# Attention with grouped heads on one core: the key order of VectorE's K transposes, and the pairs that use the wide PV

## The chip, the core and the metric

The kernel runs on one core of one Trainium2 chip. The metric is the device time of one execution in microseconds (us), and smaller is better. A core has engines that run their own instruction streams and meet through semaphores: TensorE (PE) multiplies matrices into PSUM, VectorE (DVE) and ScalarE (ACT) work on elements, GpSimd (POOL) does odd jobs, and SyncE (SP) issues the transfers between the device memory and the on-chip memory SBUF. The transfers are carried by 16 DMA engines.

## The reference

```python
B, Hq, Hkv, Sq, Sk, D = 16, 32, 8, 16, 2048, 128        # q, k, v in bf16

def reference(q, k, v):
    rep = Hq // Hkv                                      # 4 query heads share one K/V head
    k = jnp.repeat(k, rep, axis=1)
    v = jnp.repeat(v, rep, axis=1)
    scores = jnp.einsum("bhqd,bhkd->bhqk", q, k) * D ** -0.5
    p = _softmax(scores, axis=-1)
    return jnp.einsum("bhqk,bhkd->bhqd", p, v)
```

There are 16 x 8 = 128 K/V heads. Each has 2048 keys of 128 numbers and is met by 4 x 16 = 64 query rows. K and V together are 128 MB, and each of their numbers is used only by its own 64 rows.

## The kernel before

**Pairs.** Two K/V heads make a pair, so there are 64 pairs `p`. The 64 query rows of both heads fill the 128 partitions of the score tile. One pair goes through these steps:

1. SP loads 1 MB of K into `Kn` (L176) and 1 MB of V into `Vb` (L184). In `Kn` a partition holds 32 consecutive keys of one head, that is 16 keys for each of two values of `x`; in `Vb` a partition holds 16 consecutive keys of each head.
2. DVE transposes K in blocks of 32 x 32 four-byte words (function `kt`, L317, two instructions a pair, one for each `x`). A four-byte word is two neighbouring numbers of a key. The result is `KT`, in which the keys run along the free dimension. In the pattern on L318 the letters `(t b e a x)` say in which order the free dimension holds the pieces of a key's number: `t` and `e` are the index of a key within its 16 (`e` tells odd from even), `a` and `x` tell which 16, and `b` is a half of the head dimension.
3. PE multiplies `QT` with `KT` into `S_ps` (L268 and L224, 32 matmuls), 2048 scores in each of 128 rows.
4. DVE scales and negates the scores into `Sneg` in SBUF and takes the row's minimum in the same instruction (L333). It frees `S_ps`, of which there is one.
5. ACT takes exp into `P` in bf16, with the row sum (L368). Its pattern reads `Sneg` as `(n e y)` and writes `n y e`: from each group of 128 scores it takes turns between the 64 even keys and the 64 odd keys, so that an even and the following odd key lie side by side in `P` and can be moved as one four-byte word.
6. PE transposes those words of `P` in 8 blocks (L280), and ACT copies them to `PT` (L378).
7. PE multiplies `PT` with `Vb` (PV). In the wide form (L298) one matmul for each of 16 key groups uses all 128 rows of both heads as weights and both heads' V as 256 columns; half of the 128 x 256 result is of use. In the narrow form (L304) two matmuls for each key group, one for each head, with 64 rows and 128 columns, fill two halves of the array and give only what is needed. `NFAST` says how many of the last pairs use the narrow form: 12.
8. ACT multiplies by the reciprocal row sum and writes `Osb`: two instructions for the wide form (L391), one for the narrow form (L395). DVE does this for the last pair (L348). SP stores the result (L204).

Every eight pairs a new block of queries is spread by POOL (L165), transposed on PE (L246) and copied to `QT` by ACT (L358), in four parts behind four successive pairs.

**Order.** The streams of PE and ACT are written out as lists before the block: scores of pair `p + 1`, exp of pair `p`, PV and norm of pair `p - 3`, transposes of `P` of pair `p`. DVE does reduction `p`, the reciprocal of `p - 1` and the two K transposes of `p + 2`. SP issues K of step `t`, V of pair `t - 5` and the store of pair `t - 12` in one stream. There are 6 buffers for K, 8 for V and 2 for `KT`; the load of K of pair `p` waits for the transposes of pair `p - 6`, that of V for PV of pair `p - 8`. V of the last pair comes in two parts, of 12 and 4 key groups.

The lines that tie DVE's and PE's steps together are these:

```python
# PE, scores of pair p
pe.wait_ge(sem_kt, 2 * p + 2)
pe.wait_ge(sem_max, p)            # the one S_ps has been read
# DVE
dve.wait_ge(sem_s, p + 1)         # reduction of pair p
...
for g in range(2):
    kt(p + 2, g)
```

Of the kernel before, what the change touches and what calls it, by code (L numbers as in the profile page):

```python
# [5 lines left out]
ACT = mybir.ActivationFunctionType  # L6
ALU = mybir.AluOpType
BF16 = mybir.dt.bfloat16
# [5 lines left out]
NKT = 2  # L14
# [6 lines left out]
SLAG = 12  # L21
QLEAD = 7
LASTV = ((0, 12), (12, 16))
NFAST = 12


def bass_standalone__gqa_softmax__sampling_kernel(
# [12 lines left out]
    J = Sk // 128  # L40
# [13 lines left out]
    KT = [sb(f"KT{i}", [128, 2 * J * 64], F32) for i in range(NKT)]  # L54
# [3 lines left out]
    Sneg = [sb(f"Sneg{i}", [128, Sk], F32) for i in range(2)]  # L58
    P = [sb(f"P{i}", [128, Sk // 2], F32) for i in range(2)]
# [83 lines left out]
    def stage_ap(u):  # L143
        return ST_ps[:, 512 * (u % NSTAGE):512 * (u % NSTAGE + 1)]

    def o_ap(p):
        if p < NP - 3:
            return O_ps[:, 0:128]
        x = p - (NP - 3)
        return S_ps[:, 512 * x:512 * x + 128]  # L150

    with nc.Block() as block:

        @block.gpsimd
        def _(gp):
            gp.iota(iota_t[:, :], [[1, 128]], base=0, channel_multiplier=-1).then_inc(sem_id, 1)
            gp.wait_ge(sem_id, 1)
            gp.tensor_scalar(ident[:, :], iota_t[:, :], 0.0, None, op0=ALU.is_equal).then_inc(sem_id, 1)
            gp.tensor_scalar(ident4[:, :], iota_t[:, :], 0.0, None, op0=ALU.is_equal).then_inc(sem_id, 1)
            for c in range(NQC):  # L160
                gp.wait_ge(sem_q[c % NQ], 16 * (c // NQ + 1))
                if c >= 1:
                    gp.wait_ge(sem_st, last_q[c - 1, 3] + 1)
                src = Qn[c % NQ][:, :, :].rearrange("p j (b x) -> p (j b) x", b=2)
                gp.tensor_copy(  # L165
                    Q4[:, :, :, :, :].rearrange("p j b r x -> p (j b) r x"),
                    src.unsqueeze(2).to_broadcast([128, 16, 4, 64]),
                ).then_inc(sem_q4, 1)
# [51 lines left out]
        def _(pe):  # L220
# [15 lines left out]
            for op in pe_prog:  # L236
                if op[0] == "QT":
                    _, c, i, u = op
                    if i == 0:
                        pe.wait_ge(sem_q4, c + 1)  # L240
# [6 lines left out]
                    ins.then_inc(sem_st, 1)  # L247
                elif op[0] == "S":
                    _, p = op
                    pe.wait_ge(sem_kt, 2 * p + 2)  # L250
                    if p >= 1:
# [19 lines left out]
                    ins.then_inc(sem_s, 1)  # L271
                elif op[0] == "PT":
                    _, p, h, u = op
                    if h == 0:
                        pe.wait_ge(sem_exp, p + 1)
# [6 lines left out]
                elif op[0] == "PV":  # L282
# [9 lines left out]
                    for j in range(J):  # L292
                        if p == NP - 1:
                            for x, (lo, _) in enumerate(LASTV):
                                if j == lo:
                                    pe.wait_ge(sem_vl[x], 16)
                        if p < NP - NFAST:
                            ins = pe.matmul(  # L298
# [14 lines left out]
        @block.vector  # L313
        def _(dve):
            def kt(p, x):
                dve.wait_ge(sem_k[p % NK], 16 * (p // NK + 1))
                dve.transpose(  # L317
                    KT[p % NKT][:, :].rearrange("p (t b e a x) -> p x e t b a", t=J // 2, b=2, e=2, x=2)[:, x, :, :, :, :],  # L318
                    Kn[p % NK][:, :].bitcast(F32).rearrange("p (x t e b c) -> p x e t b c", x=2, e=2, b=2, c=32)[:, x, :, :, :, :],
                ).then_inc(sem_kt, 1)  # L320

            def recip(p):
                dve.wait_ge(sem_exp, p + 1)
                dve.reciprocal(rrec[:, p:p + 1], rowsum[:, p:p + 1]).then_inc(sem_rec, 1)  # L324

            for p in range(2):
                for g in range(2):
                    kt(p, g)
            for p in range(NP):
                dve.wait_ge(sem_s, p + 1)  # L330
                if p >= 2:
                    dve.wait_ge(sem_exp, p - 1)
                dve.tensor_scalar(  # L333
                    Sneg[p % 2][:, :].rearrange("p (t h x) -> p h t x", t=8, h=2),
                    S_ps[:, :].rearrange("p (h t x) -> p h t x", t=8, h=2), -scale, None,
                    op0=ALU.mult, op1=ALU.min, accum_out=nbias[:, p:p + 1],
                ).then_inc(sem_max, 1)
                if p >= 1:
                    recip(p - 1)
                if p + 2 < NP:  # L340
                    for g in range(2):
                        kt(p + 2, g)
            recip(NP - 1)
            p = NP - 1
            dve.wait_ge(sem_rec, NP)
            dve.wait_ge(sem_o[p % NO], 16 * (p // NO))
            dve.wait_ge(sem_pv, NP)
            dve.tensor_scalar(Osb[p % NO][:, :], o_ap(p), rrec[:, p:p + 1], None, op0=ALU.mult).then_inc(sem_nl, 1)  # L348

        @block.scalar  # L350
        def _(act):
            for op in act_prog:
                if op[0] == "qe":
                    _, c, i, u = op
                    act.wait_ge(sem_st, u + 1)
                    if c >= 2 and i == 0:
                        act.wait_ge(sem_s, 8 * (c - 1))
                    act.activation(  # L358
                        QT[c % 2][:, i // 2, :].rearrange("p (a x j) -> p x a j", x=2, j=4)[:, i % 2],
                        stage_ap(u).rearrange("p (j a) -> p a j", j=4), ACT.Copy,  # L360
                    ).then_inc(sem_ev, 1)
                elif op[0] == "exp":
                    _, p = op
                    act.wait_ge(sem_max, p + 1)
                    if p >= 2:
                        act.wait_ge(sem_st, last_p[p - 2, 1] + 1)

                    act.activation(  # L368
                        P[p % 2][:, :].bitcast(BF16).rearrange("p (n y e) -> p n y e", n=16, e=2),
                        Sneg[p % 2][:, :].rearrange("p (n e y) -> p n y e", n=16, e=2), ACT.Exp,  # L370
                        bias=nbias[:, p:p + 1], scale=-1.0, accum_out=rowsum[:, p:p + 1],
                    ).then_inc(sem_exp, 1)
                elif op[0] == "pe":
                    _, p, h, u = op
                    act.wait_ge(sem_st, u + 1)
                    if h == 0 and p >= NPT:
                        act.wait_ge(sem_pv, p - NPT + 1)
                    act.activation(  # L378
                        PT[p % NPT][:, 4 * h:4 * (h + 1), :].rearrange("p t q -> p (t q)"),
                        stage_ap(u), ACT.Copy,  # L380
                    ).then_inc(sem_ev, 1)
                else:
                    _, p = op
                    act.wait_ge(sem_pv, p + 1)
                    act.wait_ge(sem_rec, p + 1)
                    if p >= NO:
                        act.wait_ge(sem_o[p % NO], 16 * (p // NO))
                    if p < NP - NFAST:
                        for g in range(2):
                            rows = slice(64 * g, 64 * (g + 1))  # L390
                            ins = act.activation(Osb[p % NO][rows, :], O_ps[rows, 128 * g:128 * (g + 1)], ACT.Copy,  # L391
                                                 scale=rrec[rows, p:p + 1])
                        ins.then_inc(sem_nm, 1)
                        continue
                    act.activation(Osb[p % NO][:, :], o_ap(p), ACT.Copy,  # L395
                                   scale=rrec[:, p:p + 1]).then_inc(sem_nm, 1)
# [28 lines left out]
```

## Time and profile before

| | |
|---|---|
| time, median of 3 runs | 344.95 us (344.94 to 345.17) |
| the profiled execution: its own time | 344.92 us |
| its span, first to last instruction | 343.1 us |
| busy: PE, DVE, ACT | 312.1, 297.6, 291.8 us |
| exp, L368, 64 of them | 2481 ns each |
| K transposes, L317, 128 of them | 1218 ns each |
| reductions, L333, 64 of them | 2285 ns each |
| moved by DMA | 138.94 MB, mean 405 GB/s |

An execution takes 1.8 us more than the span that the profile covers. In the profile's rows a group is named by its line, engine, operation and tiles, with its busy time and the mean duration of one instruction; "idle before" is the time that the engine stood before instructions of the group, and the name behind the arrow says what ended it. In rows by slice each digit is a fortieth of the span. Rows in order of time begin with the start and the duration in us; a bracket gives the idle time before the instruction. Rows by stretch give the busy time of each engine, then the granted clock of PE as a share of full speed, the busy share of the DMA engines and GB/s.

### The profile page before, as it was taken

How to read it: one execution, taken by the hardware profiler on the slowest of the kernel's cores; microseconds unless marked ns; L12 is line 12 of the kernel's file. 1: busy time of each engine (PE TensorE's matmuls, PEld its weight loads, DVE VectorE, ACT ScalarE, POOL GpSimd, SP SyncE). 2: the span in 40 equal slices, each digit the busy share in tenths (PEclk: the TensorE clock that was granted, in tenths of full speed). 3: DMA queues.
4: the chain of work that ended last, by engine and by line, in shares of the span. 5: the costliest groups of instructions: out<-in, count | busy, mean ns of one | idle time of the engine just before them, and what ended most of it. 6: DMA issues, size and time to landing. Idle time of an engine off the chain costs nothing.

```text
span 343.1 us, 8217 instructions
## 1 busy us (share of the span) xinstructions
PE 312.1 (91%) x3904; PEld 189.2 (55%) x2880; DVE 297.6 (87%) x321; ACT 291.8 (85%) x404; POOL 30.3 (9%) x15
## 2 busy tenths in 40 slices
PE   0757999999999999999999999999999999887784
PEld 0413656655665575557555755665565575454354
DVE  2289989999999999999899989998999898989840
ACT  1258899999999999999999999999988899877864
POOL 4500012000400004000300004000040000000000
PEclk9999999999999999999999999999999999999999
DMA  7999999999999999999999999999999999999993
GB/s 294 429 414 415 415 411 413 414 416 417 412 418 419 413 415 417 412 420 415 412 421 414 414 416 416 415 418 417 415 412 419 419 412 420 417 413 418 410 393 126
DMA packets 37300, 138.94 MB, mean 405 GB/s; under 512 B 11408, under 2 KB 11664, under 8 KB 29072
## 3 DMA queue, kind: packets, MB, share of 16 engines
q1 hardware_dynamic: 37264, 138.42, 99.6%
q8 instruction: 27, 0.44, 0.5%
q14 instruction: 9, 0.07, 0.1%
HBM read 136.31 MB, written 2.10 MB: 403 GB/s over the span
## 4 chain that ended last, share of the span: by engine, by line
PE 83%; DMA 5%; issue 4%; DVE 3%; ACT 1%; SPq 1%; POOL 1%; DVEq 0%; ACTq 0%
PE O_ps L298 28%; PE S_ps L268 18%; PE S_ps L224 15%; PE ST_ps L280 15%; PE ST_ps L246 5%; DMA Vb<-in_v_dram 4%; DVE KT L317 2%; PE O_ps L304 2%; DMA Qn<-in_q_dram 1%; DVE Sneg L333 1%; POOL Q L165 1%; SPq L204 1%; ACT P L368 1%; SPq L184 0%; PE S_ps L304 0%
## 5 line engine op out<-in xcount | busy, mean ns | idle before, releaser
L333 DVE TENSOR_SCALAR_CACHE_REDUCE Sneg<-S_ps 128x2048 f32<-128x2048 f32 x64 | 146.2, 2285 | 25.2 <-PE S_ps L224 24.0
L368 ACT ACTIVATE P<-Sneg,nbias 128x2048 bf16<-128x2048 f32 x64 | 158.8, 2481 | 7.7 <-DVE Sneg L333 6.1
L317 DVE STREAM_TRANSPOSE KT<-Kn 128x1024 f32<-128x1024 f32 x128 | 150.9, 1218 | 10.9 <-DMA Kn<-in_k_dram 10.9
L268 PE MATMUL S_ps<-KT,QT 32*64 32x512 bf16 x1024 | 103.4, 391 | 5.5 <-DVE Sneg L333 4.7
L224 PE MATMUL S_ps<-KT,QT 32*64 32x512 bf16 x1024 | 102.0, 385 | 0.0
L298 PEld LDWEIGHTS O_ps<-Vb,PT 128*128 128x128 bf16 x832 | 77.3, 98 | 44.0 <-issue 35.7
L298 PE MATMUL O_ps<-Vb,PT 128*128 128x256 bf16 x832 | 99.9, 273 | 1.5 <-issue 1.5
L378 ACT ACTIVATE PT<-ST_ps 128x512 f32<-128x512 f32 x128 | 69.5, 595 | 6.0 <-PE ST_ps L280 4.8
L280 PE MATMUL ST_ps<-ident,P 128*128 128x128 f32 x512 | 69.0, 278 | 2.8 <-ACT P L368 2.8
L268 PEld LDWEIGHTS S_ps<-KT,QT 32*64 32x64 bf16 x1024 | 30.0, 104 | 70.4 <-issue 61.6
L280 PEld LDWEIGHTS ST_ps<-ident,P 128*128 128x128 f32 x512 | 55.1, 141 | 12.1 <-ACT P L368 9.6
L391 ACT ACTIVATE O<-O_ps,rrec 64x128 bf16<-64x128 f32 x104 | 37.7, 363 | 15.8 <-PE O_ps L298 14.7
L165 POOL COPY Q<-Qn 128x4096 bf16<-128x4096 bf16 x8 | 28.8, 3602 | 224.2 <-PE ST_ps L246 143.9
L246 PE MATMUL ST_ps<-ident,Q 128*128 128x128 f32 x128 | 20.4, 291 | 10.1 <-POOL Q L165 10.1
L358 ACT ACTIVATE QT<-ST_ps 128x512 f32<-128x512 f32 x32 | 19.3, 603 | 10.0 <-PE ST_ps L246 10.0
L246 PEld LDWEIGHTS ST_ps<-ident,Q 128*128 128x128 f32 x128 | 16.4, 150 | 10.1 <-issue 10.1
L304 PE MATMUL O_ps<-Vb,PT 128*64 128x128 bf16 x288 | 9.8, 220 | 7.2 <-issue 7.2
L304 PEld LDWEIGHTS O_ps<-Vb,PT 128*64 128x64 bf16 x288 | 8.5, 110 | 12.9 <-issue 12.9
L324 DVE RECIPROCAL rrec<-rowsum 128x1 f32<-128x1 f32 x64 | 10.1, 158 | 3.1 <-ACT P L368 3.1
L368 ACT ACTIVATION_READ_ACCUMULATOR P<-Sneg,nbias 128x1 f32 x64 | 12.2, 190 | 0.0
L395 ACT ACTIVATE O<-O_ps,rrec 128x128 bf16<-128x128 f32 x9 | 3.3, 365 | 6.6 <-PE O_ps L304 6.6
L333 DVE DVE_READ_ACCUMULATOR Sneg<-S_ps 128x1 f32 x64 | 5.3, 83 | 0.0
(12 smaller groups left out, 10.2 us busy)
## 6 DMA issues: line engine op xcount, KB each, us to landing
Kn<-in_k_dram SPq DMA_DIRECT2D x64, 1024.0 KB, 15.9
Vb<-in_v_dram SPq DMA_DIRECT2D x63, 1024.0 KB, 17.7
Qn<-in_q_dram SPq DMA_DIRECT2D x8, 256.0 KB, 15.6
out_dram<-O SPq DMA_DIRECT2D x64, 32.0 KB, 15.9
Vb<-in_v_dram SPq DMA_DIRECT2D x1, 768.0 KB, 13.0
Vb<-in_v_dram SPq DMA_DIRECT2D x1, 256.0 KB, 12.5
```

What stands on the lines that cost most here:

```text
L165: gp.tensor_copy(Q4[:, :, :, :, :].rearrange("p j b r x -> p (j b) r x"), src.unsqueeze(2).to_broadcast([128, 16, 4, 64]),).then_inc(sem_q ...
L224: return pe.add_instruction(mybir.InstMatmult(name=nc.get_next_instruction_name(), engine=mybir.EngineType.PE, ins=[pe.lower_ap(rhs), pe.l ...
L246: ins = pe.transpose(dst[:, 128 * j:128 * (j + 1)], src[:, 4 * x + j, b, :], ident4[:, :])
L268: ins = pe.matmul(s_ap, w, x, start=(acc == 0), stop=(acc == 3))
L280: ins = pe.transpose(dst[:, 128 * t:128 * (t + 1)], P[p % 2][:, 128 * x:128 * (x + 1)], ident4[:, :])
L298: ins = pe.matmul(O_ps[:, 0:256], pt[:, j // 2, j % 2, :], Vb[p % NV][:, :, j, :], start=(j == 0), stop=(j == J - 1),)
L304: ins = pe.matmul(o_ap(p)[64 * g:64 * (g + 1), :], pt[:, j // 2, j % 2, 64 * g:64 * (g + 1)], Vb[p % NV][:, g, j, :], start=(j == 0), stop ...
L317: dve.transpose(KT[p % NKT][:, :].rearrange("p (t b e a x) -> p x e t b a", t=J // 2, b=2, e=2, x=2)[:, x, :, :, :, :], Kn[p % NK][:, :].b ...
L333: dve.tensor_scalar(Sneg[p % 2][:, :].rearrange("p (t h x) -> p h t x", t=8, h=2), S_ps[:, :].rearrange("p (h t x) -> p h t x", t=8, h=2), ...
L368: act.activation(P[p % 2][:, :].bitcast(BF16).rearrange("p (n y e) -> p n y e", n=16, e=2), Sneg[p % 2][:, :].rearrange("p (n e y) -> p n ...
L378: act.activation(PT[p % NPT][:, 4 * h:4 * (h + 1), :].rearrange("p t q -> p (t q)"), stage_ap(u), ACT.Copy,).then_inc(sem_ev, 1)
L391: ins = act.activation(Osb[p % NO][rows, :], O_ps[rows, 128 * g:128 * (g + 1)], ACT.Copy, scale=rrec[rows, p:p + 1])
```

## The change

Three edits. `kt` writes the transposed keys in the order `(t b a x e)`: the even and the odd key of a couple are neighbours, and successive keys of one instruction's inner run are four words (16 bytes) apart where they were two words (8 bytes) apart. The score columns that PE computes come out in that order, so exp reads and writes straight through. And `NFAST` is 4 in place of 12: the wide PV and the norm in two instructions hold for pairs 0 to 59 in place of 0 to 51.

```diff
-NFAST = 12
+NFAST = 4
...
             def kt(p, x):
                 dve.wait_ge(sem_k[p % NK], 16 * (p // NK + 1))
                 dve.transpose(
-                    KT[p % NKT][:, :].rearrange("p (t b e a x) -> p x e t b a", t=J // 2, b=2, e=2, x=2)[:, x, :, :, :, :],
+                    KT[p % NKT][:, :].rearrange("p (t b a x e) -> p x e t b a", t=J // 2, b=2, e=2, x=2)[:, x, :, :, :, :],
                     Kn[p % NK][:, :].bitcast(F32).rearrange("p (x t e b c) -> p x e t b c", x=2, e=2, b=2, c=32)[:, x, :, :, :, :],
                 ).then_inc(sem_kt, 1)
...
                     act.activation(
-                        P[p % 2][:, :].bitcast(BF16).rearrange("p (n y e) -> p n y e", n=16, e=2),
-                        Sneg[p % 2][:, :].rearrange("p (n e y) -> p n y e", n=16, e=2), ACT.Exp,
+                        P[p % 2][:, :].bitcast(BF16), Sneg[p % 2][:, :], ACT.Exp,
                         bias=nbias[:, p:p + 1], scale=-1.0, accum_out=rowsum[:, p:p + 1],
                     ).then_inc(sem_exp, 1)
```

## The prediction

> **What bounds the kernel now.** I read four views, in this order: the page's rows by slice and its groups, the busy time by stretch, the order of time in the middle of the run, and the order of time at its end.
>
> First the rows by slice, and the stretches of the middle.
>
> ```profile
> DMA  7999999999999999999999999999999999999993
> GB/s 294 429 414 415 415 411 413 414 416 417 412 418 419 413 415 417 412 420 415 412 421 414 414 416 416 415 418 417 415 412 419 419 412 420 417 413 418 410 393 126
> ```
> ```profile
> 100.00:150.00 50.00, 50.00 (x594) 30.23 (x423) 47.55 (x52) 46.90 (x65) 3.60 (x1) 1.00 1.02 416
> ```
>
> The 16 DMA engines are busy in every slice from the second to the last but one, at 411 to 421 GB/s for most of them. The kernel must move 138.9 MB, so DMA by itself fills the span from about 2 us to 339 us. In the same stretch VectorE (DVE) is busy for 47.55 of 50 us, ScalarE (ACT) for 46.90 and TensorE (PE) for 50.00. Four resources are nearly full at once; which of them has room has to be read in the order of time. Here are VectorE and then ScalarE in the middle, for one pair of heads without a Q transpose:
>
> ```profile
> 105.32 2.29 DVE L333 TENSOR_SCALAR_CACHE_REDUCE Sneg<-S_ps 128x2048 f32<-128x2048 f32 x1
> 107.54 0.08 DVE L333 DVE_READ_ACCUMULATOR Sneg<-S_ps 128x1 f32 x1
> 107.54 0.16 DVE L324 RECIPROCAL rrec<-rowsum 128x1 f32<-128x1 f32 x1
> 107.62 2.35 DVE L317 STREAM_TRANSPOSE KT<-Kn 128x1024 f32<-128x1024 f32 x2
> 109.97 2.29 DVE L333 TENSOR_SCALAR_CACHE_REDUCE Sneg<-S_ps 128x2048 f32<-128x2048 f32 x1
> ```
> ```profile
> 104.29 2.48 ACT L368 ACTIVATE P<-Sneg,nbias 128x2048 bf16<-128x2048 f32 x1
> 106.67 0.19 ACT L368 ACTIVATION_READ_ACCUMULATOR P<-Sneg,nbias 128x1 f32 x1
> 107.17 0.74 ACT L391 ACTIVATE O<-O_ps,rrec 64x128 bf16<-64x128 f32 x2 [0.31 <-PE O_ps L298]
> 107.93 1.09 ACT L378 ACTIVATE PT<-ST_ps 128x512 f32<-128x512 f32 x2
> ```
>
> VectorE runs without a gap from 105.32 to 109.97: 4.65 us for a pair, of which 2.35 are the two K transposes. A pair's reduction cannot begin before the transposes in front of it on VectorE are done. ScalarE repeats at 104.29 and 109.05. So VectorE sets the pace of the pairs without a Q transpose, and nothing hides a longer transpose there. The room is elsewhere, at the end:
>
> ```profile
> 315.54 1.08 PE L304 MATMUL O_ps<-Vb,PT 128*64 128x128 bf16 x32 [0.99 <-issue]
> 320.64 1.09 PE L304 MATMUL O_ps<-Vb,PT 128*64 128x128 bf16 x32 [0.99 <-issue]
> 326.88 1.08 PE L304 MATMUL O_ps<-Vb,PT 128*64 128x128 bf16 x32 [2.14 <-issue]
> ```
> ```profile
> 318.04 2.37 DVE L317 STREAM_TRANSPOSE KT<-Kn 128x1024 f32<-128x1024 f32 x2 [0.45 <-DMA Kn<-in_k_dram]
> 323.14 2.37 DVE L317 STREAM_TRANSPOSE KT<-Kn 128x1024 f32<-128x1024 f32 x2 [0.47 <-DMA Kn<-in_k_dram]
> ```
> ```profile
> 326.19 12.98 DMA Vb<-in_v_dram
> ...
> 339.30 1.10 PE S_ps L304 x32
> ```
>
> Here compute has caught up with the loads. VectorE waits 0.45 us for each K, PE stands 1 to 2 us before each PV, and the pairs come every 5.1 us, which is DMA's pace for 2.1 MB at 416 GB/s. The chain of waits ends with the last V (12.98 us of transfer), PV of the last pair at 339.30, 3.8 us before the end. The end is DMA's, and compute arrives in time with a reserve. The question is how large that reserve is for VectorE.
>
> **The reserve.** VectorE's first reduction starts at 18.17 us, its last (pair 63) at 330.95: 312.8 us. Back to back it needs 62 steps of 4.65 us and one, the last, without transposes, which is bounded by the single S buffer: 2.3 for the reduction, 1.9 for the scores and 0.2 of signals, 4.4 us. That is 292.7 us, a reserve of 20.1 us, or 0.32 us a pair, or **0.16 us for each transpose** of 1.22 us (13%). Below that a longer transpose disappears under DMA. Above it each 0.1 us on a transpose costs 12.4 us.
>
> **The change, part by part.** Transposes: the same 128 instructions with the same elements. In the old layout a run writes every second 4-byte word (8 bytes apart), in the new one every fourth (16 bytes apart). Nothing in this trace shows a write 16 bytes apart on VectorE, so I bound it. Lower end: nothing, since ScalarE's QT copy (L358), which reads PSUM at a step of 512 bytes, took 603 ns against 595 for PT's contiguous one (L378). A gain is excluded: from the transpose's 1218 ns for 1024 elements to the reduction's 2285 ns for 2048, which writes in contiguous runs, the slope is 1.04 ns an element, so that the stepped write costs nothing now that could be saved. Nearest row for a charge: the exp, the one SBUF access here that leaves a short stretch with every element (its two innermost reads are 256 bytes apart). It took 2481 ns for 2048. What it would take contiguously is bounded by ScalarE's other rows: from 128 elements in 365 ns (L395) to 512 in 595 the slope is 0.60 ns an element, which would make 365 + 1920 x 0.60 = 1517 ns; at the other end the step costs nothing. The step's charge is thus 0 to 0.47 ns an element. I take the middle, 0.24 ns, since neither end has a row of its own: on 1024 elements 0.25 us, a transpose of 1.46 us. The bound by exp is 0.48 us; a far bound is that each element takes its 1.04 ns twice, another 1.07 us.
>
> [...]
>
> Exp: the same 64 instructions, now contiguous on both sides. By the bounds above they take 2.48 to 1.52 us, by the same middle 2.0. Off the path: VectorE keeps 4.65 us whatever ScalarE saves. What the saving does lift is the pairs with a Q transpose, where ScalarE has 4.65 + 0.60 us and the chain shows 5.1 to 5.2 us a pair: ScalarE's need falls to about 4.8.
>
> PV of pairs 52 to 59: 16 wide matmuls (1.92 us in the groups by time) for 32 narrow ones (1.09 us), so PE +0.8 us a pair, and ScalarE's norm 0.74 instead of 0.37. I cost it at nothing: PE stands 0.99 us before each of these PVs. If VectorE sets the pace at over 5 us, the first 52 pairs show that PE manages the wide form in 4.65. Pair 59 lies among the last instructions: its PV begins at 330.84 and would end 0.8 later, the transposes of P of pair 62 and exp of pair 63 follow by 0.5 to 0.7, which a shorter exp gives back and PV 63's wait of 0.73 us for V covers. Without either cover it costs 0.7 us. No DMA or queue is moved; SP's V loads wait for PV 8 pairs back, which is done 14 us before the issue of the last one.
>
> **The sum.** With 0.25 us a transpose the pair takes 4.65 + 0.50 = 5.15 us in VectorE, over ScalarE's 4.8 and the 5.1 that DMA needs. The last reduction starts at 18.2 + 62 x 5.15 + 4.4 = 341.9 us. From there to the end, as before without the wait for V: 7.6 us to the last PV (330.95 to 338.57, where PV 62 ends), less 0.5 for the exp, and 3.8 behind it. Span 352.8 against 343.1, so +9.7 us. The profiled execution took 344.92 us, 1.8 outside its span; the median of the runs is 344.95, the same. Forecast **355 us**. With exp's bound of 0.48 us: 5.61 us a pair, 370.4 + 10.9, span 381.3, time 383.
>
> **Rivals.** *The write costs nothing, or under 0.16 us, and DMA sets the end as before.* For it: the QT copy's 8 ns, and that exp's excess may be ScalarE's own. Against: it needs the charge in the lower third of its bounds. It ends on the other side of my forecast, not slower: 344.9 us, with 0.5 either way from the tail just described. The point of decision is a transpose of 1.38 us. *Twice the time for each element*: a transpose of 2.29 us, a pair of 6.79, the last reduction at 443.6 and the time at 456 us. For it: no row of before writes single words so far apart; against: exp, which leaves its stretch with every element too, stays at 1.21 ns an element in all, far from doubled. *A gain*: ScalarE's shorter exp lets compute catch up earlier than 264 us, where PE first waits for a load. Worth little, as the loads do not start earlier for it. In the last 7 us the DMA share falls to 0.70, 0.62 and 0.60, idle time that amounts to 2.1 us of full pace; if a calmer end closed it, 342.8 us. *That the change does not do what it says* is possible for the exp alone: if it keeps 2.48 us, the forecast rises by 0.5 us and the rival of no change by 0.2.
>
> **How the numbers follow.** Charge as forecast, a transpose of over 1.38 and up to 1.70 us: 0.43. DMA as before: 0.31, of it 0.27 within 0.2% and 0.02 each side. Twice, or near it: 0.16. A gain: 0.08. A small loss at the end alone: 0.02. About 0.2% (0.7 us) is what a measurement of this kernel can tell from no change. Faster: 0.08 + 0.02 = 0.10; the same: 0.27; slower: 0.43 + 0.16 + 0.02 + 0.02 = 0.63. The range takes in the case of no change and the forecast's up to exp's bound, 344 to 383; it leaves out the doubled case and most of the gain. The forecast case alone runs from 346 to 383.
>
> **What would show it.** The group of L317: 1.46 us right, 1.22 the rival, 2.29 the doubling. The group of L368: about 2.0. In the middle VectorE without gaps at 5.15 us a pair, with ScalarE idle beside it; SP's waits for K's transposes grow, and DMA falls below 411 GB/s. At the end PV of the last pair waits for ScalarE, not for V. If L317 stays below 1.38 us and the time still moves by over 1 us, or if the transposes lengthen and VectorE nonetheless shows gaps, my reading is wrong.

## The result

The changed kernel takes 407.86 us (median of 6 runs, 406.07 to 408.05) against 345.06 us before (344.63 to 345.54): a ratio of 1.180, 95% interval 1.178 to 1.183. It is slower, as forecast, but by 62.8 us where the forecast had 10, and outside the range of 344 to 383.

The groups of the page after, in the page's own columns (busy time, mean ns of one, idle time before):

```profile
L317 DVE STREAM_TRANSPOSE KT<-Kn 128x1024 f32<-128x1024 f32 x128 | 261.2, 2228 | 5.6 <-DMA Kn<-in_k_dram 5.6
L333 DVE TENSOR_SCALAR_CACHE_REDUCE Sneg<-S_ps 128x2048 f32<-128x2048 f32 x64 | 159.8, 2497 | 7.1 <-PE S_ps L224 7.1
...
L368 ACT ACTIVATE P<-Sneg,nbias 128x2048 bf16<-128x2048 f32 x64 | 128.2, 2003 | 15.3 <-DVE Sneg L333 13.3
```

The transposes went from 1218 to 2228 ns; exp fell from 2481 to 2003. VectorE was busy for 297.6 us and is now busy for 384.6. Its order of time in the middle shows what a pair costs:

```profile
101.95 2.33 DVE L333 TENSOR_SCALAR_CACHE_REDUCE Sneg<-S_ps 128x2048 f32<-128x2048 f32 x1
104.15 0.14 DVE L333 DVE_READ_ACCUMULATOR Sneg<-S_ps 128x1 f32 x1
104.15 0.22 DVE L324 RECIPROCAL rrec<-rowsum 128x1 f32<-128x1 f32 x1
104.22 3.96 DVE L317 STREAM_TRANSPOSE KT<-Kn 128x1024 f32<-128x1024 f32 x2
107.98 2.33 DVE L333 TENSOR_SCALAR_CACHE_REDUCE Sneg<-S_ps 128x2048 f32<-128x2048 f32 x1
...
110.26 3.96 DVE L317 STREAM_TRANSPOSE KT<-Kn 128x1024 f32<-128x1024 f32 x2
113.97 2.36 DVE L333 TENSOR_SCALAR_CACHE_REDUCE Sneg<-S_ps 128x2048 f32<-128x2048 f32 x1
```

Reductions start at 101.95, 107.98 and 113.97: VectorE is never idle, and a pair takes about 5.98 us (6.03 and 5.99 here, 5.97 at 383 us) where it took 4.65. The difference of 1.33 us is 0.665 us for each transpose. The recorded durations overlap the next instruction (104.22 + 3.96 is 108.18, and the next reduction starts at 107.98), so the pace, not the mean of 2228 ns, is the price. It is somewhat more than that: 4.65 us was the pace at which PE let VectorE run, and VectorE alone needed 4.53 us a pair (see The reserve), which makes 0.72 us for each transpose.

Everything else now waits for VectorE. The waits of SP's queue say so, and so does the share of DMA in the slices:

```profile
SPq L176 <- DVE KT L317: 259.9, 58, 10.2
```
```profile
GB/s 320 419 417 412 417 417 399 355 392 342 358 354 361 375 353 374 342 370 354 362 357 378 367 362 358 361 349 372 364 362 350 373 356 345 366 388 263 96 8 18
```

SP stood 259.9 us before its K loads until transposes freed a buffer (53.4 us before). Until about 60 us the loads still run at 412 to 419 GB/s, into free buffers; then they fall to VectorE's pace, and they are finished near 380 us, more than 20 us before the end.

### The profile page after: what moved, and what is told of

Same layout as the page of the kernel before. It is cut to its first block, busy times and chain, and to the rows that moved or that the text cites. A ratio compares the mean times of both kernels' runs of the same rounds, so it can differ in the third digit from the quotient of the medians.

```text
span 406.0 us, 7969 instructions
## 1 busy us (share of the span) xinstructions
PE 319.7 (79%) x3776; PEld 203.2 (50%) x2752; DVE 384.6 (95%) x321; ACT 265.5 (65%) x412; POOL 30.3 (7%) x15
## 4 chain that ended last, share of the span: by engine, by line
DVE 76%; issue 17%; PE 4%; DMA 1%; POOL 1%; ACT 0%; SPq 0%; DVEq 0%; ACTq 0%
DVE Sneg L333 39%; DVE KT L317 36%; DMA Qn<-in_q_dram 1%; DVE rrec L324 1%; PE ST_ps L246 1%; POOL Q L165 1%; PE S_ps L268 1%; PE S_ps L304 1%; PE S_ps L224 1%; PE ST_ps L280 0%; PE O_ps L298 0%; PE O_ps L304 0%; ACT QT L358 0%; SPq L176 0%; DVE O L348 0%
## 5 line engine op out<-in xcount | busy, mean ns | idle before, releaser
L317 DVE STREAM_TRANSPOSE KT<-Kn 128x1024 f32<-128x1024 f32 x128 | 261.2, 2228 | 5.6 <-DMA Kn<-in_k_dram 5.6
L333 DVE TENSOR_SCALAR_CACHE_REDUCE Sneg<-S_ps 128x2048 f32<-128x2048 f32 x64 | 159.8, 2497 | 7.1 <-PE S_ps L224 7.1
L268 PE MATMUL S_ps<-KT,QT 32*64 32x512 bf16 x1024 | 109.2, 394 | 72.3 <-DVE Sneg L333 62.7
L368 ACT ACTIVATE P<-Sneg,nbias 128x2048 bf16<-128x2048 f32 x64 | 128.2, 2003 | 15.3 <-DVE Sneg L333 13.3
L298 PE MATMUL O_ps<-Vb,PT 128*128 128x256 bf16 x960 | 115.3, 273 | 0.0
L298 PEld LDWEIGHTS O_ps<-Vb,PT 128*128 128x128 bf16 x960 | 89.1, 98 | 48.8 <-issue 39.3
L390 ACT ACTIVATE O<-O_ps,rrec 64x128 bf16<-64x128 f32 x120 | 43.5, 363 | 104.6 <-PE O_ps L298 103.8
L224 PE MATMUL S_ps<-KT,QT 32*64 32x512 bf16 x1024 | 109.4, 390 | 0.0
L268 PEld LDWEIGHTS S_ps<-KT,QT 32*64 32x64 bf16 x1024 | 36.5, 105 | 135.7 <-issue 128.6
L324 DVE RECIPROCAL rrec<-rowsum 128x1 f32<-128x1 f32 x64 | 24.4, 381 | 3.5 <-ACT P L368 3.5
L333 DVE DVE_READ_ACCUMULATOR Sneg<-S_ps 128x1 f32 x64 | 19.6, 306 | 0.0
```

The lines of the kernel that those rows point to most:

```text
L224: return pe.add_instruction(mybir.InstMatmult(name=nc.get_next_instruction_name(), engine=mybir.EngineType.PE, ins=[pe.lower_ap(rhs), pe.l ...
L268: ins = pe.matmul(s_ap, w, x, start=(acc == 0), stop=(acc == 3))
L298: ins = pe.matmul(O_ps[:, 0:256], pt[:, j // 2, j % 2, :], Vb[p % NV][:, :, j, :], start=(j == 0), stop=(j == J - 1),)
L317: dve.transpose(KT[p % NKT][:, :].rearrange("p (t b a x e) -> p x e t b a", t=J // 2, b=2, e=2, x=2)[:, x, :, :, :, :], Kn[p % NK][:, :].b ...
L333: dve.tensor_scalar(Sneg[p % 2][:, :].rearrange("p (t h x) -> p h t x", t=8, h=2), S_ps[:, :].rearrange("p (h t x) -> p h t x", t=8, h=2), ...
L368: act.activation(P[p % 2][:, :].bitcast(BF16), Sneg[p % 2][:, :], ACT.Exp, bias=nbias[:, p:p + 1], scale=-1.0, accum_out=rowsum[:, p:p + 1 ...
```

## Experiments

### Which part of the change it is

Three kernels each take one part of the change into the kernel before.

The pairs with the narrow PV:

```diff
-NFAST = 12
+NFAST = 4
```

> The kernel before with one edit: the narrow PV for the last 4 pairs only. Theory (the transposes' write step is the whole cause): no part of the 62.8 us is from here; the pairs come at DMA's pace with PE standing about 1 us before each of these PVs, so 344.5 to 345.7 us. Rival (the wide PV and the norm in two instructions hold up the last pairs): 8 pairs times 0.8 us on PE or 0.37 us on ScalarE, 348 to 351 us.

Measured: 344.71 us (11 runs), ratio 0.9991 (0.9982 to 1.0). No cost. At the end PE still stands before the wide PV of pairs that had the narrow one, in the order of time of this kernel:

```profile
300.12 1.91 PE L298 MATMUL O_ps<-Vb,PT 128*128 128x256 bf16 x16 [0.43 <-issue]
305.20 1.91 PE L298 MATMUL O_ps<-Vb,PT 128*128 128x256 bf16 x16 [0.37 <-issue]
310.31 1.91 PE L298 MATMUL O_ps<-Vb,PT 128*128 128x256 bf16 x16 [0.41 <-issue]
```

The idle time of about 1 us before each was the cover that the prediction named; about 0.4 us of it is left.

The key order of K alone, with the old exp (the keys in `P` are then not in V's order):

```diff
-    ...rearrange("p (t b e a x) -> p x e t b a", ...)
+    ...rearrange("p (t b a x e) -> p x e t b a", ...)
```

> The kernel before with one edit: the K transposes write in the new order (words 16 bytes apart); exp still reads with its step, so that the keys in P are not in V's order. Theory: VectorE alone sets the pace, so the transposes take 1.85 to 2.25 us, a pair 6.0 us, and the time is 406 to 410 us, although exp stays at 2.48 us. Rival (the slower transposes come from the shorter exp or from what runs beside them, such as ScalarE's reads without a step): transposes near 1.22 us and 345 us.

Measured: 406.2 us, ratio 1.177 (1.174 to 1.180); transposes 2261 ns, exp 2501 ns. This one line carries 61.2 of the 62.8 us.

Exp alone (again with `P`'s keys not in V's order):

```diff
-    P[p % 2][:, :].bitcast(BF16).rearrange("p (n y e) -> p n y e", n=16, e=2),
-    Sneg[p % 2][:, :].rearrange("p (n e y) -> p n y e", n=16, e=2), ACT.Exp,
+    P[p % 2][:, :].bitcast(BF16), Sneg[p % 2][:, :], ACT.Exp,
```

> The kernel before with one edit: exp reads and writes straight through, K stays in the old order, so that the keys in P are not in V's order. Theory: exp at 2.00 us as in the changed kernel, transposes at 1.22 us, pairs with a Q transpose come somewhat faster in the middle, and DMA sets the end: 344.3 to 345.3 us. Rival (ScalarE's share of the pace is worth time): under 344 us.

Measured: 345.07 us, ratio 0.9999 (0.999 to 1.0008); exp 2003 ns, transposes 1219 ns. Saving 0.48 us on ScalarE for each pair, 30.6 us in all, moves the time by nothing: VectorE waits longer for K instead (16.8 us in all, where kernels with the old exp wait 10.9 to 14.0).

### How the price goes with the step

Four kernels vary only how far apart the transposes write successive words. The first writes them side by side (`P`'s keys not in V's order). Two spread `KT` with unused words, with the kernel's results as before. The last interleaves the halves of the head dimension too. The pattern in which PE reads `KT` follows where the layout needs it.

```diff
-    "p (t b e a x) -> p x e t b a"
+    "p (t b e x a) -> p x e t b a"            # 4 bytes
+    "p (t b e a z) -> p z e t b a", z=3       # 12 bytes, x is z = 0 and 1; z=4: 16 bytes
+    "p (t a x e b) -> p x e t b a"            # 32 bytes, with exp straight through
```

> The kernel before with one edit: the K transposes write each run of 32 words side by side (4 bytes apart); the keys in P are then not in V's order. All theories: a transpose of 1.17 to 1.25 us and 345 us. If it were shorter than 1.17 us, the old step of 8 bytes had a cost too, which the forecast excluded.

> The kernel before with the transposed K spread out: every couple of words is followed by an unused third, so that the transposes write words 12 bytes apart; the order of keys and the result are those of before. Theory A (the charge comes when consecutive writes share no 16-byte stretch; at 12 bytes one in four still does): most of the charge, a transpose of 1.6 to 1.9 us and about 375 to 410 us. Theory B (up to below 16 bytes a step is free): 1.22 us and 345 us. PE's moving read is spread out as well; its matmuls are expected to stay at 391 ns.

> The kernel before with the transposed K spread out by two unused words after every couple: the step of the changed kernel (16 bytes), but the old order of keys, exp with its step, and each 16-byte stretch is written by two instructions and not by two passes of two. One V buffer fewer (7), for space. Theory (the step itself is charged): a transpose as in the changed kernel, 1.85 to 2.25 us, about 406 us. Rival (the four passes over the same 16 bytes of the changed kernel's order are charged): 1.22 to 1.5 us, under 360 us.

> The changed kernel's key order with both halves of the head dimension interleaved as well: the transposes write words 32 bytes apart, exp reads straight through, PE reads its columns 8 bytes apart. Theory A (a charge for each write that begins a new 16-byte stretch): as at 16 bytes, 1.85 to 2.25 us a transpose and about 407 us. Theory B (the charge grows with the step): over 2.4 us and over 430 us.

The cleanest measure is at the start of each run, when the first K has come and PE has not begun with scores (PE and ScalarE do nothing from 2 to 10 us, and then only the Q transposes). In the order of time of VectorE, the kernel before first, then the changed kernel, and steps of 12, 16 (spread) and 32 bytes:

```profile
5.66 2.37 DVE L317 STREAM_TRANSPOSE KT<-Kn 128x1024 f32<-128x1024 f32 x2 [5.66 <-DMA Kn<-in_k_dram]
```
```profile
5.64 7.53 DVE L317 STREAM_TRANSPOSE KT<-Kn 128x1024 f32<-128x1024 f32 x4 [5.64 <-DMA Kn<-in_k_dram]
```
```profile
5.63 2.93 DVE L317 STREAM_TRANSPOSE KT<-Kn 128x1024 f32<-128x1024 f32 x2 [5.63 <-DMA Kn<-in_k_dram]
```
```profile
5.62 7.55 DVE L317 STREAM_TRANSPOSE KT<-Kn 128x1024 f32<-128x1024 f32 x4 [5.62 <-DMA Kn<-in_k_dram]
```
```profile
5.71 7.64 DVE L317 STREAM_TRANSPOSE KT<-Kn 128x1024 f32<-128x1024 f32 x4 [5.71 <-DMA Kn<-in_k_dram]
```

Divide by the count: 1.19 us at 8 bytes, 1.46 at 12, 1.88 and 1.89 at 16, 1.91 at 32. At 4 bytes the same two instructions take 2.37 us as at 8, and the group's mean is 1217 ns (1218 at 8). Taking off the 0.12 us that the old transpose has beyond 1024 words at 1.04 ns, a word costs 1.04 ns up to 8 bytes, 1.31 at 12, 1.72 at 16 and 1.75 at 32. So the price comes on between 8 and 16 bytes and then stays. One number fits the three steps that cost something: about 1.75 ns for each 16-byte stretch begun (16 bytes, since the price is about the same at 16 and 32 and three quarters of it at 12). At 12 bytes four words begin three stretches (1.31 each), from 16 bytes on every word begins one. At 8 bytes two words share a stretch; that would be 0.87 ns each, less than the 1.04 that was measured. The price is the step's: it is there with the old key order too, and before anyone reads `KT`, so it is no collision with PE's reads. Nor is it one with the loads: at 385.61 us in the changed kernel, where DMA moves only 6 GB/s, the next reduction still starts 3.68 us after the first of two transposes. The 12-byte step was expected at 1.6 to 1.9 us by theory A, and 1.46 us is the measure here (the group's mean is 1.53). So neither theory holds as it was written: there is a charge, but it is 0.27 of the 0.70 us and not most of it. The price for each stretch gives that; an extra charge for each change of stretch, three in four words, would make it 0.52 us.

The times of these kernels taught a second thing. 4 bytes gave 345.04 us, as expected, but 12 bytes gave 391.96, 16 (spread) 446.32 and 32 bytes 446.16, where the last two should have matched the changed kernel's 407. There VectorE waits:

```profile
156.49 2.29 DVE L333 TENSOR_SCALAR_CACHE_REDUCE Sneg<-S_ps 128x2048 f32<-128x2048 f32 x1 [0.77 <-PE S_ps L224]
...
163.37 2.29 DVE L333 TENSOR_SCALAR_CACHE_REDUCE Sneg<-S_ps 128x2048 f32<-128x2048 f32 x1 [0.76 <-PE S_ps L224]
```

That is the spread 16-byte kernel, at 6.88 us for a pair with a Q transpose. Its score matmuls are slower, because PE reads the spread `KT` too. In the order of time of PE, four matmuls a row, before and then here:

```profile
153.09 0.39 PE L268 MATMUL S_ps<-KT,QT 32*64 32x512 bf16 x4
153.31 0.39 PE L224 MATMUL S_ps<-KT,QT 32*64 32x512 bf16 x4
153.54 0.39 PE L268 MATMUL S_ps<-KT,QT 32*64 32x512 bf16 x4
```
```profile
154.01 0.63 PE L224 MATMUL S_ps<-KT,QT 32*64 32x512 bf16 x4
154.46 0.63 PE L268 MATMUL S_ps<-KT,QT 32*64 32x512 bf16 x4
154.91 0.63 PE L224 MATMUL S_ps<-KT,QT 32*64 32x512 bf16 x4
```

Rows start 0.225 us apart before and 0.45 us apart here; the 12-byte kernel has 0.34. With 512 columns a row that is 0.44, 0.88 and 0.66 ns a column. Four, two and eight-thirds columns lie in a 16-byte stretch: 1.76, 1.76 and 1.77 ns for each. My expectation that PE would not mind (391 ns a matmul; 622 and 507 were measured) was wrong. What this does to the time can be worked out from PE's stream in the kernel before, which has no gap in the middle. One round of PV, transposes of `P` and scores takes 4.65 us, from 105.21 to 109.86:

```profile
105.21 1.92 PE L298 MATMUL O_ps<-Vb,PT 128*128 128x256 bf16 x16
106.97 1.04 PE L280 MATMUL ST_ps<-ident,P 128*128 128x128 f32 x8
107.94 0.42 PE L268 MATMUL S_ps<-KT,QT 32*64 32x512 bf16 x4
...
109.86 1.92 PE L298 MATMUL O_ps<-Vb,PT 128*128 128x256 bf16 x16
```

Eight rows of scores that are each 0.225 us longer make it 6.45 us, and 6.44 is what a pair without a Q transpose takes in the spread 16-byte kernel. At 12 bytes 4.65 + 8 x 0.115 is 5.57, and 5.56 was measured. So PE's stream sets the pace in these three kernels, and their total times say nothing on VectorE. It also means that the 4.65 us of the kernel before are the length of PE's round.

### Moving the order to another engine

If the write of K must not be spread, someone else can put even and odd keys side by side. PE can, by the order in which it reads `KT`:

```diff
-    kt = KT...rearrange("p (t b y e) -> p b e t y", ...)
+    kt = KT...rearrange("p (t b o w e) -> p b e t w o", ...)      # o: even, odd
```

> The kernel before, with the order of the keys changed by PE's read in place of VectorE's write: K stays in the old order (words 8 bytes apart), the score matmuls read their moving columns in turns from the even and the odd keys (128 words apart in bf16 terms), and exp reads straight through. The result is the reference's. Theory A (a read that leaves its 16-byte stretch with each column costs PE nothing): score matmuls at 391 ns, exp 2.00 us, transposes 1.22 us, 344.3 to 345.3 us. Theory B (it costs PE as exp's step costs ScalarE, by a quarter or more): score matmuls over 480 ns each, a pair's scores 2.3 us or more in place of 1.8, so that VectorE waits and the time goes over 347 us.

Measured: 492.97 us, ratio 1.429 (1.427 to 1.431). Theory B, and more: 703 ns a matmul, rows 0.54 us apart, 1.05 ns a column where it was 0.44. The same sum for PE's round, 4.65 + 8 x 0.315, gives 7.17 us a pair without a Q transpose, and 7.16 was measured. VectorE's reduction waits 179.3 us in all for PE.

Or VectorE's reduction can, which then writes `Sneg` 8 bytes apart. The order of the two heads' key blocks moves into exp as runs of 128:

```diff
-    Sneg[p % 2][:, :].rearrange("p (t h x) -> p h t x", t=8, h=2),
-    S_ps[:, :].rearrange("p (h t x) -> p h t x", t=8, h=2), -scale, None,
+    Sneg[p % 2][:, :].rearrange("p (n y e) -> p n e y", n=16, e=2),
+    S_ps[:, :].rearrange("p (n e y) -> p n e y", n=16, e=2), -scale, None,
```

> The kernel before, with the order of the keys changed by VectorE's reduction: it writes Sneg with words 8 bytes apart (even and odd keys side by side), the K transposes stay as before, and exp reads runs of 128 straight. The result is the reference's. Theory (8 bytes are free for any VectorE write): reduction 2.29 us, exp 2.00 us, transposes 1.22 us, 344.3 to 345.3 us. Rival (the reduction pays for a step at all): over 2.5 us and over 350 us.

Measured: 344.99 us, ratio 0.9998 (0.9988 to 1.0008); reduction 2283 ns, exp 2003, transposes 1218. This is the change's aim without its price: exp loses its step and nobody pays. It gains no time, since DMA sets the end (VectorE waits 15.8 us for K in all).

The same reduction with words 16 bytes apart (the keys of `P` not in V's order) asks whether the price is the transpose's alone:

```diff
+    Sneg[p % 2][:, :].rearrange("p (n q f) -> p n f q", n=16, f=4),
+    S_ps[:, :].rearrange("p (n f q) -> p n f q", n=16, f=4), -scale, None,
```

> The kernel before with one edit: the reduction writes Sneg with words 16 bytes apart, the transposes of K as before; the keys in P are then not in V's order. Theory A (the charge of about 0.65 ns for each word written 16 bytes apart is VectorE's, for any instruction): reduction of 3.4 to 3.8 us, a pair of 5.8 to 6.1 us, 395 to 412 us. [...]

Measured: 420.22 us. Its first reduction, with nothing queued in front of it, in the order of time:

```profile
18.27 3.74 DVE L333 TENSOR_SCALAR_CACHE_REDUCE Sneg<-S_ps 128x2048 f32<-128x2048 f32 x1 [7.00 <-PE S_ps L224]
```

3.74 us, less 0.155 of fixed time (2.285 us before, less 2048 x 1.04 ns), is 1.75 ns for each of 2048 words: theory A, close to the price in the transposes, in an instruction of another kind that reads PSUM. The pace is 6.14 us a pair (386.8 us from the first reduction to the last), just over the expected range, and the time lies 8 us over it.

### The reserve

Two kernels use the new order, with its exp, for one pair in eight and for one in two.

```diff
+    order = "t b a x e" if p % 8 == 0 else "t b e a x"      # 2 in place of 8 in the second
```

> The kernel before, with the new key order (and exp straight through) for one pair in eight, the old order for the others. The result is the reference's. Theory (the reserve of 20.1 us that VectorE has under DMA swallows what the slow transposes add: 8 pairs times 1.33 us, that is 5.98 less 4.65): 10.6 us more on VectorE, 344.3 to 345.7 us. Rival (VectorE sets the end already, or a late K delays the loads behind it): 350 to 356 us.

> The same with the new order for every second pair. Theory: 32 times 1.33 us is 42.6 us, 22.5 us over the reserve; the pairs with a Q transpose that keep the old order are still held by ScalarE (5.2 us where VectorE needs 4.65, 16 of them, up to 8 us more): 366 to 375 us. Rival (no reserve): 387 us.

Measured: 344.89 us, ratio 0.9995 (0.9986 to 1.0004), and 364.34 us, ratio 1.054 (1.052 to 1.057). With eight slow pairs VectorE's 10.6 us more leave no trace in the time. Most of it is made up at once: the two pairs behind a slow one take 4.54 to 4.57 us each, so that eight pairs take 39.96 us in the middle (69.46 to 109.42) where they took 39.48. The rest vanishes under DMA: VectorE still waits for K at the end, 0.47 us before one of the last transposes.

```profile
318.04 2.37 DVE L318 STREAM_TRANSPOSE KT<-Kn 128x1024 f32<-128x1024 f32 x2 [0.47 <-DMA Kn<-in_k_dram]
```

With 32 of them, pairs alternate:

```profile
153.58 2.26 DVE L334 TENSOR_SCALAR_CACHE_REDUCE Sneg<-S_ps 128x2048 f32<-128x2048 f32 x1
...
158.13 2.24 DVE L334 TENSOR_SCALAR_CACHE_REDUCE Sneg<-S_ps 128x2048 f32<-128x2048 f32 x1
...
164.12 2.26 DVE L334 TENSOR_SCALAR_CACHE_REDUCE Sneg<-S_ps 128x2048 f32<-128x2048 f32 x1
```

That is 4.55 and 5.99 us, without a gap on VectorE. The fast pairs take less than the 4.65 us of the kernel before, although their instructions are the same: PE has waited for VectorE in the slow pair (1.21 us at 156.00) and no longer holds it up. The kernel before shows that pace too, at its start, where PE has no PV to do yet and waits 0.9 us for VectorE in each pair:

```profile
27.22 2.25 DVE L333 TENSOR_SCALAR_CACHE_REDUCE Sneg<-S_ps 128x2048 f32<-128x2048 f32 x1
...
31.75 2.25 DVE L333 TENSOR_SCALAR_CACHE_REDUCE Sneg<-S_ps 128x2048 f32<-128x2048 f32 x1
```

So VectorE by itself needs 4.53 us a pair. A slow pair adds about 1.46 us to a fast one here, and 31 of them lie between the first reduction and the last: 45 us were added, and 19.2 (364.34 less 345.12, measured beside it) arrived. The reserve is about 26 us. The trace of before gives nearly that with 4.53 in place of 4.65: 312.8 less 62 x 4.53 + 4.4 is 27.5, where the prediction had read 20.1. The extra 8 us that I allowed for ScalarE in the Q pairs did not come, since a slow and a fast pair together take about 10.55 us, more than two Q pairs took before (5.14 to 5.19 each). That is why the time lies just under the range.

## Why the prediction was wrong

*The bound: right at the end, misread in the middle.* DMA sets the end with a reserve for VectorE under it, as the two mixed kernels show, and after the change VectorE runs without gaps. But the 4.65 us were not VectorE's. They are PE's round, and VectorE, which needs 4.53, was held to it; its transposes, whose recorded durations elsewhere reach 0.07 us into the next instruction, end at 109.97 just where the reduction starts, so that no gap is seen. The row of the middle had PE busy for 50.00 of 50 us. The prediction's base is thus 0.12 us a pair too long, some 7 us over the run, and its reserve as much too short. Beside the price of the write that is little.

*The price of the write: wrong, and it decided.* The failed step is "The step's charge is thus 0 to 0.47 ns an element. I take the middle, 0.24 ns". The way was right, a longer transpose that VectorE cannot hide; the term was mis-sized. The transposes pay 0.68 ns a word, 0.70 us each, at the start of the run. In the pace it is 0.72 us each against VectorE's own 4.53 (0.665 against 4.65), where the sum had 0.25 and the range ended at 0.48. With the measured pace the prediction's own sum gives 18.2 + 62 x 5.98 + 4.4 = 393.4 us for the last reduction (394.43 in the trace, where the last step took 5.1 us and not 4.4), 10.9 behind it and 1.8 outside the span: 406 us, against 407.9.

*Why the row misled.* The excess of exp came out as said, 478 ns or 0.233 ns an element; that was luck, since 0.24 was only the middle of two bounds. But it is another pattern. Exp takes turns between two runs of scores and so uses each 16 bytes four times before it moves on; a transpose never returns within its pass. That this is why exp paid a third of the price is argued from the patterns and not shown: no run has ScalarE read one word of each stretch, and its price for a stretch may simply be lower. PE's read in turns, which cost 1.05 ns a column, lies between the old 0.44 and the 1.76 that a whole stretch costs, which fits. The prediction saw that no row had single words 16 bytes apart, and still let the nearest row end its range; the rival of twice the time (1.07 us) bounded the truth from above, and most of the stretch between 383 and 456 us was given to neither case.

*Exp and its saving: right.* 2.0 us was said, by the same lucky middle, and 2003 ns measured. That it is worth nothing in the time held for a reason that was given: VectorE or DMA sets the end.

*PV and the norm: right.* No cost, and the idle time of PE was the cover.

*The rivals.* DMA as before fell with the transpose at over 1.38 us. Twice the time put 1.07 us on a transpose where 0.70 (at the start) and 0.72 (in the pace) were measured. The gain from a calmer end did not appear in any of the three kernels with the shorter exp or fewer narrow PVs (344.71 to 345.07 us).

## What to carry to other kernels

Count how many 16-byte stretches an access begins, not only its elements: on VectorE's writes and PE's moving reads a stretch cost about 1.75 ns here. VectorE's four-byte words were free up to 8 bytes apart (1.19 us a transpose at the start, 2283 ns a reduction), and 16 bytes apart they cost 0.70 us on a transpose; PE took 0.44 ns a column with four columns in a stretch and 0.88 with two. The count is not the whole of it: a read in turns, which comes back to a stretch, cost PE less for each change (1.05 ns against 1.76) but more than its stretches alone (0.44). When an order must change, put the step where it stays within that, as the reduction with words 8 bytes apart did for nothing. And when no row of a trace shows an access, do not let the nearest row of another engine end the range: ask how often the pattern comes back to the same bytes. Last, an engine without a gap in its rows need not set the pace: add up the round of the other engine that is busy all the time.

## What was not expected of the hardware

PE's moving read has the same price for a stretch as VectorE's write: 1.76 ns against 1.75. In these runs the old layout was just at the limit, with four columns a stretch: PV's read of V, with eight columns a stretch, is no faster (16 x 256 columns in the 1.76 us from 105.21 to 106.97, 0.43 ns each), and at two the score matmuls start 0.45 us apart in place of 0.225.

In the changed kernel VectorE's ends fall behind its starts. The reductions start every 5.98 us throughout, but they end later and later:

```profile
50.22 0.07 DVE L333 DVE_READ_ACCUMULATOR Sneg<-S_ps 128x1 f32 x1
```
```profile
385.53 0.73 DVE L333 DVE_READ_ACCUMULATOR Sneg<-S_ps 128x1 f32 x1
```

The accumulator's read takes 0.07 us at 50 us and 0.73 at 385, and the reduction 2.26 and 2.92; once a gap of 2.1 us comes, at 394 us, they are back at 0.08 and 2.29. In the spread 16-byte kernel, where VectorE pauses 0.33 to 0.77 us a pair, they stay at 0.08 and 2.29, and with the new order in every second pair, without a pause, at 0.07 and 2.26. The lag grows by some 12 ns a pair ((0.73 - 0.07) us over 56 pairs), is gone after a pause, and does not build up where every second pair has the old order. That writes queue up would look like this; it is a guess that no run tests.
